# Attention stage of a fused attention and feed-forward kernel: every product takes more than 64 rows and 128 columns of the array

## The chip, the cores and the metric

The kernel runs on one core of one Trainium2 chip. The metric is the device time of one execution in microseconds (us), lower is better. The core has TensorE (PE), with its weight loads shown as PEld, VectorE (DVE), ScalarE (ACT), GpSimd (POOL), and SyncE (SP), which here issues almost all DMAs, in order.

## The reference

Three stages in float32: causal attention with a bias from a running sum of `s`, a feed-forward with softplus, and a normalised, gated feed-forward. Only the first is touched.

```python
# q, k, v: (4, 8, 576, 64); s: (4, 8, 576)
scores = scale * np.matmul(q, k.transpose(0, 1, 3, 2))
s_pos = np.maximum(s, 0.0)
cum = np.cumsum(s_pos, axis=-1)
bias = -(cum[:, :, :, None] - cum[:, :, None, :])
scores = np.where(causal, -1000000000.0, scores + np.minimum(bias, 0.0))
scores = scores - np.max(scores, axis=-1, keepdims=True)
attn = np.exp(scores)
attn = attn / (np.sum(attn, axis=-1, keepdims=True) + 1e-09)
return np.matmul(attn, v).astype(np.float32)
...
x = np.ascontiguousarray(attn_out.transpose(0, 2, 1, 3)).reshape(B * S, H * D)
x = _moe_ref(x=x, **moe_kwargs)
return _moe2_ref(x=x, **moe2_kwargs)
```

## The kernel before

There are 32 heads of 576 positions and 64 channels, worked in 16 pairs. The queries of a head stand in blocks 0 to 3 of 128, and the last 64 queries of both heads of a pair stand together in one block 4 (tile `e4`: rows 0 to 63 the even head, 64 to 127 the odd one). The order of the work is a table of numbers, `OFF`: each step has an offset, an event of head n stands at n plus that offset, all events are sorted, and each engine gets its instructions in that order. Nothing is scheduled afterwards: every engine works its list from the top, waiting where it must. A *slot* is the work between one head's steps and the same steps of the next. Even heads carry the steps of a pair.

The steps of one head, with their names in the table:

- LD, LV: SP loads q, k and v of a pair (L338, L345, L348). QT: TensorE transposes q, then k (`kn`), 96 rows at a time (L357). QH and QL split them into two float32r parts (`hl`), on ACT and DVE.
- QD: SP copies parts of `hl` into the stacked operand `sk` (three DMAs of 256 KB, L381), and four rows of the running sum beside them (L382). QB does the same for block 4: `a8`, 8 rows (L387), and `bd`.
- S0, S1: scores of blocks 0 to 3 (L418, L419, 68 and 128 rows) with the causal mask (L420). S4: scores of block 4 of the pair: a product of `a8`, which has 8 rows (L427), three with `bd` (L428 to L430) and the mask (L431), for columns 0 to 255 and again for 256 to 575.
- M, E, R, N: row maximum (DVE), exponential (ACT), reciprocal (DVE), scaling (POOL, L472).
- T0 to T3: TensorE transposes the weights `e` to PSUM (`pt`, two buffers, shared by all four). T0 and T1 are the six blocks of early queries. T2 and T3 are the late queries (blocks 3 and 4): each block of 128x128 (L504) is followed by one of `e4` in which the head has only 64 rows (L501).
- H copies `pt` to SBUF (ACT, L515), and L takes the remainder (DVE, L521): `ph`, `pl`.
- V0: early queries times v in float32 (L530); the stationary operand is one head's 64 columns, so its output stands in 64 partitions, and both heads share one PSUM tile, `o0`. Each product shows as two in the trace. V1: late queries times v in float32r, eight products over 128 keys and two over the last 64 keys (L539).
- OX, OC, OF, WS, WT: copies out of PSUM and stores of the two parts of the output, `x` (L565) and `xb` (L569).

In the same order stand twelve chunks of the first feed-forward's weights, one per pair for the first twelve pairs: a fetch of 512 KB (`raw`, L222), the conversion, and the split. After the attention the two feed-forwards follow.

Of the kernel before, what the change touches and what calls it, by code (L numbers as in the profile page):

```python
# [8 lines left out]
F32 = mybir.dt.float32  # L9
F32R = mybir.dt.float32r  # L10
# [4 lines left out]
AF = mybir.ActivationFunctionType  # L15
ALU = mybir.AluOpType
# [66 lines left out]
    "V1": 3.16992,  # L83
    "OC": 3.43645,
    "OF": 4.01001,
    "OX": 2.90176,
    "WS": 3.80066,
    "WT": 4.18994,
    "C0": 0.26268,
# [51 lines left out]
def attention_moe_kernel(ctx, tc, q, k, v, s, w_in, w_out, w_gate, w_val, w_out2, rms_g, out):  # L141
    nc = tc.nc
    B, H, S, D = q.shape
# [3 lines left out]
    P = 128  # L147
# [4 lines left out]
    T = 384  # L152
# [19 lines left out]
    pools = {}  # L172
# [4 lines left out]
    def ps_p(name):  # L177
        return ps.tile([P, 512], F32, tag="p", name=name, bufs=2)

    def ps_1(tag, w=512):  # L180
        return ps.tile([P, w], F32, tag=tag, name=tag, bufs=1)

    def f32(ap):
        return ap.bitcast(F32)

    ident = const.tile([P, P], F32, tag="ident", name="ident")
    ident16 = const.tile([P, P], BF16, tag="ident16", name="ident16")
    mask16 = const.tile([P, P], BF16, tag="mask16", name="mask16")
    mask64 = const.tile([P, 64], BF16, tag="mask64", name="mask64")
    bds = []  # L190
    ones = const.tile([P, P], F32R, tag="ones", name="ones")
    gcol = const.tile([P, KD], F32, tag="gcol", name="gcol")
    aug = dram.tile([NH, 4, 2, S], F32R, tag="aug", name="aug")
    aug4 = dram.tile([NH, 4, P + S], F32R, tag="aug4", name="aug4")
# [146 lines left out]
    def a_loadv(p):  # L341
        b, h = pair_bh(p)
        t = pools["nat"].tile([P, NB, 2, D], F32, tag="vn", name="vn", bufs=3)
        for hd in range(2):
            nc.sync.dma_start(  # L345
                out=t[:, 0:4, hd, :],
                in_=v[b, h + hd, 0:512, :].rearrange("(c p) d -> p c d", p=P))
        nc.sync.dma_start(  # L348
            out=t[:, 4], in_=v[b, h:h + 2, 448:576, :].rearrange("h p d -> p h d"))
        st["vn", p] = t  # L350

    def a_qt(p, which):
# [30 lines left out]
        st["sk", n] = sk  # L383

    def a_qb(p):
        a8 = pools["stack"].tile([8, P + S], F32R, tag="a8", name="a8", bufs=2)
        nc.sync.dma_start(out=f32(a8), in_=f32(aug4[2 * p:2 * p + 2]).rearrange("h r n -> (h r) n"))  # L387
        bd, hl = bds[p % 2], st["hl", p]
        for r in (slice(0, 64), slice(64, P)):
            nc.vector.tensor_copy(out=bd[r, :, r], in_=f32(hl[r, 0:2, 512:S]))  # L390
        st["a8", p] = a8

    def a_vh(p):
        vn = st["vn", p]
# [11 lines left out]
    EO = {0: 0, 1: 128, 2: 384, 3: 768}  # L406
# [13 lines left out]
            nc.tensor.matmul(t[:, c + w - P:c + w], ident16, mask16, start=False, stop=True)  # L420

    def a_s4(p):
        a8, bd, hl = st.pop(("a8", p)), bds[p % 2], st["hl", p]
        t = st["s4", p] = ps_s("s4")[:, 0:256], ps_s("s4")[:, 0:320]
        for o, j0, w in ((t[0], 0, 256), (t[1], 256, 320)):
            j = slice(j0, j0 + w)
            nc.tensor.matmul(o, a8[:, 0:P], a8[:, P + j0:P + j0 + w], start=True, stop=False)  # L427
            nc.tensor.matmul(o, bd[:, 0], hl[:, 2, j], start=False, stop=False)  # L428
            nc.tensor.matmul(o, bd[:, 0], hl[:, 3, j], start=False, stop=False)
            nc.tensor.matmul(o, bd[:, 1], hl[:, 2, j], start=False, stop=(j0 == 0))  # L430
        nc.tensor.matmul(t[1][:, 256:320], ident16, mask64, start=False, stop=True)  # L431
# [47 lines left out]
    def a_n4(p):  # L479
        scale_rows(st["e4", p], st["r4", p])  # L480

    # groups of transposed blocks: (key block, query blocks); the first two feed float32 products
    GRP = [
        [(0, [0, 1, 2])],
        [(1, [1, 2]), (2, [2])],
        [(0, [3, 4]), (1, [3, 4]), (4, [4])],
        [(2, [3, 4]), (3, [3, 4])],
    ]
    GW = [384, 384, 448, 384]
    IS = 384  # L490

    def a_t(n, g):
        e, e4, hd = st["e", n], st["e4", n // 2], n % 2
        t = ps_p("pt")
        o = 0
        for jb, ibs in GRP[g]:
            j0 = B0[jb]
            for ib in ibs:
                if ib == 4:
                    r = slice(hd * 64, hd * 64 + 64)  # L500
                    nc.tensor.transpose(t[:, o:o + 64], e4[r, j0:j0 + P], ident[r, r])  # L501
                    o += 64
                else:
                    nc.tensor.transpose(t[:, o:o + P], e[:, EO[ib] + j0:EO[ib] + j0 + P], ident)  # L504
                    o += P
        st["pt", n, g] = t[:, 0:o]

    def a_h(n, g):
        t = st["pt", n, g]
        if g == 0:  # L510
            st["p0", n] = pools["pp"].tile([P, 768], F32, tag="p0", name="p0")
        if g == 2:
            st["ph", n] = pools["pp"].tile([P, 832], F32R, tag="ph", name="ph")
        dst = st["p0", n][:, 384 * g:384 * g + 384] if g < 2 else st["ph", n][:, 448 * (g - 2):448 * (g - 2) + GW[g]]
        nc.scalar.activation(out=dst, in_=t, func=AF.Copy)  # L515

    def a_l(n, g):
        if g == 2:
            st["pl", n] = pools["pp"].tile([P, 832], F32R, tag="pl", name="pl")
        c = slice(448 * (g - 2), 448 * (g - 2) + GW[g])  # L520
        nc.vector.tensor_tensor(out=st["pl", n][:, c], in0=st["pt", n, g], in1=f32(st["ph", n][:, c]), op=ALU.subtract)  # L521

    def a_v0(n):
        p, hd = divmod(n, 2)
        if hd == 0:
            st["o0", p] = ps_1("o0")
        o = st["o0", p][hd * D:(hd + 1) * D]
        vn, x = st["vn", p], st["p0", n]
        for jb, (c, w) in enumerate(((0, 384), (384, 256), (640, 128))):
            nc.tensor.matmul(o[:, IS - w:IS], vn[:, jb, hd, :], x[:, c:c + w], start=(jb == 0), stop=(jb == 2))  # L530

    def a_v1(n):
        p, hd = divmod(n, 2)
        vs = st["vs", p]
        t = st["o1", n] = st["x1"][:, 256:448]
        for i, x in enumerate((st["ph", n], st["pl", n])):
            for jb, c in ((0, 0), (1, 192), (2, 448), (3, 640), (4, 384)):
                r, w = (slice(0, P), 192) if jb < 4 else (slice(64, P), 64)
                nc.tensor.matmul(t[:, 192 - w:192], vs[r, jb, 2 * hd:2 * hd + 2, :].rearrange("p a d -> p (a d)"),  # L539
                                 x[r, c:c + w], start=(i == 0 and jb == 0), stop=(i == 1 and jb == NB - 1))  # L540

    def halves(hd):
        return (slice(0, 64), slice(64, P)) if hd == 0 else (slice(64, P), slice(0, 64))

    def a_ox(p):
        st["x", p] = pools["xo"].tile([P, IS], F32, tag="x", name="x")
        nc.scalar.activation(out=st["x", p], in_=st.pop(("o0", p))[:, 0:IS], func=AF.Copy)

    def a_oc(n):
        a, b_ = halves(n % 2)  # L550
# [20 lines left out]
    def on_pair(fn, hd):  # L571
        def run(n):
            p = n // 2
            if n % 2 == hd and p < NP:
                fn(p)
        return run
# [5 lines left out]
        "R": a_r, "QB": on_pair(a_qb, 0), "S4": on_pair(a_s4, 0), "M4": on_pair(a_m4, 0), "E4": on_pair(a_e4, 0),  # L582
        "R4": on_pair(a_r4, 0), "N4": on_pair(a_n4, 0),
        "N0": lambda n: a_n(n, 0), "N1": lambda n: a_n(n, 1),
        **{f"T{g}": (lambda n, g=g: a_t(n, g)) for g in range(4)},
        **{f"H{g}": (lambda n, g=g: a_h(n, g)) for g in range(4)},
        **{f"L{g}": (lambda n, g=g: a_l(n, g)) for g in range(2, 4)},
        "V0": a_v0, "V1": a_v1, "OC": a_oc, "OF": a_of,
        "OX": on_pair(a_ox, 1), "WS": on_pair(a_ws, 1), "WT": on_pair(a_wt, 1),
        "LD": on_pair(a_load, 0), "LV": on_pair(a_loadv, 0),  # L590
        "QT": lambda n: a_qt(n // 2, n % 2), "QH": lambda n: a_qh(n // 2, n % 2), "QL": lambda n: a_ql(n // 2, n % 2), "QD": a_qd,
        "VH": on_pair(a_vh, 0), "VL": on_pair(a_vl, 0),
# [242 lines left out]
    with tc.manual_schedule():  # L835
        nc.scalar.preload_act_table_set("natural_log_exp_and_others")
        with ExitStack() as es:
# [6 lines left out]
            for c in range(NA):  # L844
                x = OFF["C0"] + OFF["CR"] * c
# [13 lines left out]
        with ExitStack() as es0:  # L859
# [15 lines left out]
            x = OFF1["P0"]  # L875
# [5 lines left out]
            for v in sorted({STEPS[i][0] for i in NS}):  # L881
                i = min(i for i in NS if STEPS[i][0] == v)
                t, n = v % NTILE, FA if v < NTILE else F1 - FA
                if v > 0:
                    for a in range(KD):
                        x = i + OFF1["xs"] + OFF1["xt"] * a
                        at(x + OFF1["xl"], x_load, v, a)
                        at(x, x_split, v, a, nc.gpsimd)
                e = i + n - 1 + OFF1["Y"]
# [6 lines left out]
                x = "5" if t == NTILE - 1 else ""  # L896
# [9 lines left out]
            for c in range(NA, 3 * F2):  # L906
                x = OFF2["L0"] + OFF2["LR"] * c
# [49 lines left out]
```

## Time and profile before

| | |
|---|---|
| time, three runs | 1238.71, 1239.92, 1243.12 us; median 1239.92 |
| profiled execution | span 1242.4 us from the first to the last instruction; no other time of it is listed |
| PE busy | 1176.2 us (95%), 6404 products |
| DVE, ACT, POOL busy | 771.7, 617.7, 471.5 us |
| mean granted TensorE clock | 0.989 of full speed |
| attention's products | from 5.5 us to 314.6 us of the span |

The profiled execution's span is inside the range of the three runs, 2.5 us over the median. Busy times of PE come from a model of pipelined products: a product shown as 0.27 us long may be followed by the next after 0.11 us. What a product really takes is the step from its start to the next one's start.

### The profile page before, as it was taken

Reading aid. Unit: us, or ns where it says so; the run is one execution under the profiler, and the core shown is the slowest. Engines: PE = TensorE matmul, PEld = TensorE weight load, DVE = VectorE, ACT = ScalarE, POOL = GpSimd, SP = SyncE. Lnnn points to the kernel's source line nnn. Section 1 sums busy time; section 2 is a strip of 40 time slices with the busy share of each in tenths; the row PEclk is TensorE's granted clock in tenths of the full one; section 3 lists DMA queues with packets and bytes.
Section 4 is the critical chain, followed back from the end, with each engine's and each line's share of the span. In section 5 each row is a group of like instructions: output and inputs, shape, how many; then the busy total and the mean of one; then the engine's idle time right before and its main releaser. Section 6 shows DMA issues by size and latency. Waiting matters only on the chain.

```text
span 1242.4 us, 18308 instructions
## 1 busy us (share of the span) xinstructions
PE 1176.2 (95%) x6404; PEld 1042.1 (84%) x6404; DVE 771.7 (62%) x1396; ACT 617.7 (50%) x1467; POOL 471.5 (38%) x487
## 2 busy tenths in 40 slices
PE   4999999999999998999989879999999999999998
PEld 3677777776988888999888768899999999999997
DVE  4666676654699999998999999533333332333322
ACT  2667666665677777866666666442121121212111
POOL 4455655543354544346576776762000000000000
PEclk9999999999899998999999999999999999999999
DMA  9998888753333343544452332331101010010000
GB/s 181 198 192 178 200 193 186 167 131 100 99 129 119 122 139 123 162 140 134 159 165 91 120 101 85 117 97 58 39 14 39 14 39 1 14 39 13 26 1 26
DMA packets 139037, 128.96 MB, mean 104 GB/s; under 512 B 66656, under 2 KB 116352, under 8 KB 138912
## 3 DMA queue, kind: packets, MB, share of 16 engines
q1 hardware_dynamic: 138848, 127.74, 38.6%
q8 instruction: 51, 0.84, 0.3%
q14 instruction: 42, 0.34, 0.1%
q0 software_dynamic: 96, 0.04, 0.0%
HBM read 76.46 MB, written 26.12 MB: 83 GB/s over the span
## 4 chain that ended last, share of the span: by engine, by line
PE 67%; DVE 22%; ACT 4%; issue 3%; DMA 2%; SPq 2%; POOL 1%; DVEq 0%; POOLq 0%; ACTq 0%
DVE gl L694 5%; PE x L539 4%; PE pt L504 4%; PE g L644 4%; PE g L643 4%; PE v L644 4%; PE v L643 4%; PE v L642 4%; PE g L642 4%; PE o L530 4%; DVE l L685 4%; DVE e L677 3%; PE o L818 3%; PE o L819 3%; PE o L817 3%
## 5 line engine op out<-in xcount | busy, mean ns | idle before, releaser
L643 PE MATMUL y<-gl,w 128*128 128x384 f32 x384 | 134.5, 350 | 25.4 <-DVE gl L694 24.1
L252 POOL TENSOR_TENSOR wf<-ur 128x512 int32<-128x512 int32 x68 | 94.3, 1386 | 123.7 <-DVE ur L246 34.1
L802 DVE TENSOR_TENSOR u<-g,u 128x384 f32<-128x384 f32 x71 | 39.5, 556 | 158.9 <-ACT u L801 158.9
L642 PE MATMUL y<-gh,w 128*128 128x384 f32 x384 | 130.8, 341 | 3.1 <-ACT l L669 1.4
L644 PE MATMUL y<-gh,w 128*128 128x384 f32 x384 | 130.6, 340 | 0.0
L472 POOL TENSOR_SCALAR e<-e,r 128x256 f32<-128x256 f32 (+2 forms) x144 | 78.3, 560 | 127.9 <-ACT hl L368 103.1
L804 ACT ACTIVATE gh<-l 128x384 fp32r<-128x384 f32 x72 | 37.8, 524 | 156.0 <-DVE l L803 156.0
L801 ACT ACTIVATE u<-g 128x384 f32<-128x384 f32 x71 | 34.8, 490 | 151.9 <-PE g L644 151.8
L643 PEld LDWEIGHTS y<-gl,w 128*128 128x128 f32 x384 | 73.3, 191 | 36.7 <-DVE gl L694 35.1
L643 PE MATMUL g<-xl,w 128*128 128x384 f32 x284 | 95.6, 336 | 1.8 <-DVE xl L636 1.8
L689 ACT ACTIVATE gh<-l 128x384 fp32r<-128x384 f32 x96 | 49.9, 520 | 93.7 <-DVE l L685 93.5
L642 PE MATMUL g<-xh,w 128*128 128x384 f32 x284 | 95.8, 337 | 0.7 <-ACT xh L635 0.7
L694 DVE TENSOR_TENSOR gl<-l,gh 128x384 fp32r<-128x384 f32 x90 | 93.1, 1035 | 4.5 <-ACT gh L689 0.7
L644 PE MATMUL g<-xh,w 128*128 128x384 f32 x284 | 95.9, 338 | 0.0
L642 PE MATMUL h<-xh,w 128*128 128x384 f32 x256 | 89.2, 348 | 6.8 <-DVE e L681 6.6
L642 PE MATMUL v<-xh,w 128*128 128x384 f32 x284 | 94.9, 334 | 0.0
L644 PE MATMUL v<-xh,w 128*128 128x384 f32 x284 | 94.9, 334 | 0.0
L643 PE MATMUL v<-xl,w 128*128 128x384 f32 x284 | 94.9, 334 | 0.0
L643 PE MATMUL h<-xl,w 128*128 128x384 f32 x256 | 88.4, 345 | 3.5 <-POOL xl L639 3.3
L644 PE MATMUL h<-xh,w 128*128 128x384 f32 x256 | 87.4, 341 | 0.0
L685 DVE TENSOR_TENSOR l<-l,e 128x384 f32<-128x384 f32 x96 | 84.0, 875 | 3.7
L677 DVE SCALAR_TENSOR_TENSOR e<-u,e 128x384 f32<-128x384 f32 x96 | 73.9, 770 | 17.1 <-ACT l L669 17.1
(191 smaller groups left out, 3281.7 us busy)
## 6 DMA issues: line engine op xcount, KB each, us to landing
sk<-hl SPq DMA_DIRECT2D x96, 256.0 KB
raw<-in_moe_w_out_dram SPq DMA_DIRECT2D x28, 512.0 KB
raw<-in_moe_w_in_dram SPq DMA_DIRECT2D x16, 512.0 KB
raw<-in_moe_w_gate_dram SPq DMA_DIRECT2D x12, 512.0 KB
raw<-in_moe_w_val_dram SPq DMA_DIRECT2D x12, 512.0 KB
wf<-wf SPq DMA_DIRECT2D x24, 256.0 KB
wl<-wf SPq DMA_DIRECT2D x24, 256.0 KB
xr<-x SPq DMA_DIRECT2D x28, 192.0 KB
```

The lines of the kernel that those rows point to most:

```text
L252: nc.gpsimd.tensor_tensor(out=w.bitcast(I32), in0=u, in1=r3, op=ALU.add)
L472: nc.gpsimd.tensor_scalar(out=e, in0=e, scalar1=r, scalar2=1.0, op0=ALU.mult, op1=ALU.mult)
L504: nc.tensor.transpose(t[:, o:o + P], e[:, EO[ib] + j0:EO[ib] + j0 + P], ident)
L530: nc.tensor.matmul(o[:, IS - w:IS], vn[:, jb, hd, :], x[:, c:c + w], start=(jb == 0), stop=(jb == 2))
L539: nc.tensor.matmul(t[:, 192 - w:192], vs[r, jb, 2 * hd:2 * hd + 2, :].rearrange("p a d -> p (a d)"), x[r, c:c + w], start=(i == 0 and jb = ...
L642: nc.tensor.matmul(o, wh, xh, start=start, stop=False)
L643: nc.tensor.matmul(o, wh, xl, start=False, stop=False)
L644: nc.tensor.matmul(o, wl, xh, start=False, stop=stop)
L677: nc.vector.scalar_tensor_tensor(out=e, in0=st.pop(("u", i)), scalar=-1.0, in1=e, op0=ALU.add, op1=ALU.subtract)
L685: nc.vector.tensor_tensor(out=l, in0=l, in1=st.pop(("e", i)), op=ALU.add)
L689: nc.scalar.activation(out=gh, in_=st["l", i], func=AF.Copy)
L694: eng.tensor_tensor(out=gl, in0=st.pop(("l", i)), in1=f32(st["gh", i]), op=ALU.subtract)
```

## The change

All products of the attention now cover more than 64 rows of the array and all 128 columns. The late queries of a pair's block 4 are transposed once for both heads (T3 becomes a step of the pair, four transposes of 128x128; the fifth, over the last key block, is added to T0 of the odd head, in the same PSUM tile). `ph` and `pl` become tiles of the pair, two new steps H4 and L4 copy that fifth block. V0 takes the columns of both heads as its stationary operand and uses one half of its output; its copy OX is made once a head, 64 partitions each. `a8` is two fixed tiles of 128 rows, zeroed once, of which 8 are loaded. The last key block of v holds 64 zero rows above its 64 loaded rows (a POOL memset a pair, and a smaller DMA), so that V1 runs over 128 rows there too. Comments are dropped, and lines move by up to 21.

```diff
-    "OX": 2.90176,
+    "OX": 2.45,
+    "H4": 1.94275,
+    "L4": 1.9428,
...
+            a8 = pools["stack"].tile([P, P + S], F32R, tag=f"a8{i}", name=f"a8{i}", bufs=1)
+            a8s.append(a8)
+            nc.gpsimd.memset(f32(a8), 0.0)
...
+        nc.gpsimd.memset(t[0:64, 4], 0.0)
         nc.sync.dma_start(
-            out=t[:, 4], in_=v[b, h:h + 2, 448:576, :].rearrange("h p d -> p h d"))
+            out=t[64:P, 4], in_=v[b, h:h + 2, 512:S, :].rearrange("h p d -> p h d"))
...
-        a8 = pools["stack"].tile([8, P + S], F32R, tag="a8", name="a8", bufs=2)
-        nc.sync.dma_start(out=f32(a8), in_=f32(aug4[2 * p:2 * p + 2]).rearrange("h r n -> (h r) n"))
+        a8 = a8s[p % 2]
+        nc.sync.dma_start(out=f32(a8[0:8]), in_=f32(aug4[2 * p:2 * p + 2]).rearrange("h r n -> (h r) n"))
...
     def a_t(n, g):
-        e, e4, hd = st["e", n], st["e4", n // 2], n % 2
+        e = st["e", n]
...
-                if ib == 4:
-                    r = slice(hd * 64, hd * 64 + 64)
-                    nc.tensor.transpose(t[:, o:o + 64], e4[r, j0:j0 + P], ident[r, r])
-                    o += 64
-                else:
-                    nc.tensor.transpose(t[:, o:o + P], e[:, EO[ib] + j0:EO[ib] + j0 + P], ident)
-                    o += P
+                c = EO[ib] + B0[jb]
+                nc.tensor.transpose(t[:, o:o + P], e[:, c:c + P], ident)
+                o += P
+        if g == 0 and n % 2:
+            nc.tensor.transpose(t[:, o:o + P], st["e4", n // 2][:, B0[4]:S], ident)
+            st["pt", n - 1, 4] = t[:, o:o + P].rearrange("p (h q) -> p h q", h=2)
         st["pt", n, g] = t[:, 0:o]
+    def a_t4(p):
+        t = ps_p("pt")
+        for jb in range(4):
+            nc.tensor.transpose(t[:, jb * P:(jb + 1) * P], st["e4", p][:, B0[jb]:B0[jb] + P], ident)
+        st["pt", 2 * p, 3] = t.rearrange("p (b h q) -> p b h q", b=4, h=2)
...
     def a_v0(n):
...
-        o = st["o0", p][hd * D:(hd + 1) * D]
+        o = st["o0", n] = ps_1("o0")
...
-            nc.tensor.matmul(o[:, IS - w:IS], vn[:, jb, hd, :], x[:, c:c + w], start=(jb == 0), stop=(jb == 2))
+            nc.tensor.matmul(o[:, IS - w:IS], vn[:, jb].rearrange("p h d -> p (h d)"), x[:, c:c + w],
+                             start=(jb == 0), stop=(jb == 2))
...
     def a_v1(n):
...
-                r, w = (slice(0, P), 192) if jb < 4 else (slice(64, P), 64)
-                nc.tensor.matmul(t[:, 192 - w:192], vs[r, jb, 2 * hd:2 * hd + 2, :].rearrange("p a d -> p (a d)"),
-                                 x[r, c:c + w], start=(i == 0 and jb == 0), stop=(i == 1 and jb == NB - 1))
+                c = slice(0, W3) if jb < 4 else slice(P, W3)
+                nc.tensor.matmul(t[:, c], vs[:, jb, 2 * hd:2 * hd + 2, :].rearrange("p a d -> p (a d)"),
+                                 x[:, jb, hd, c], start=(i == 0 and jb == 0), stop=(i == 1 and jb == NB - 1))
...
+    def a_ox(n):
+        p, hd = divmod(n, 2)
+        if hd == 0:
+            st["x", p] = pools["xo"].tile([P, IS], F32, tag="x", name="x")
+        r = slice(hd * D, (hd + 1) * D)
+        nc.scalar.activation(out=st["x", p][r], in_=st.pop(("o0", n))[r, 0:IS], func=AF.Copy)
```

TensorE, an even head's slot from T2 to V1. In these lists a digit behind a name is the number of a buffer, and sizes are those of the output. Before:

```order
L504 MATMUL pt<-ident,e 128x128
L501 MATMUL pt<-ident,e_2067 128x64
L504 MATMUL pt<-ident,e 128x128
L501 MATMUL pt<-ident,e_2067 128x64 x2
L530 MATMUL o_2138<-p_2117,vn 64x384
L530 MATMUL o_2138<-p_2117,vn 64x256
L530 MATMUL o_2138<-p_2117,vn 64x128
L504 MATMUL pt<-ident,e 128x128
L501 MATMUL pt<-ident,e_2067 128x64
L504 MATMUL pt<-ident,e 128x128
L501 MATMUL pt<-ident,e_2067 128x64
L539 MATMUL x_188<-ph,vs 128x192 x4
```

And now, the same place (in an odd head's slot the four rows of L513, block 4 of the pair, are not there):

```order
L503 MATMUL pt<-ident,e 128x128 x4
L545 MATMUL o_3777<-p_3758,vn 128x384
L545 MATMUL o_3777<-p_3758,vn 128x256
L545 MATMUL o_3777<-p_3758,vn 128x128
L513 MATMUL pt<-ident,e_3726 128x128 x4
L555 MATMUL x_192<-ph,vs 128x192 x4
L555 MATMUL x_192<-ph,vs 128x64
```

Full and half transposes no longer alternate; nothing else moved on TensorE except the one transpose that joins T0 of odd heads.

GpSimd at the program's start. Before:

```order
L298 MEMSET bd_133 128x256
L298 MEMSET bd_135 128x256
L310 MEMSET rows 32x576 x4
L312 MEMSET zero 32x256
L315 DMA aug_82<-zero 16x4x64 x2
```

And now:

```order
L300 MEMSET bd_133 128x256
L303 MEMSET a_135 128x704
L300 MEMSET bd_137 128x256
L303 MEMSET a_139 128x704
L315 MEMSET rows 32x576 x4
L317 MEMSET zero 32x256
L320 DMA aug_82<-zero 16x4x64 x2
```

Two memsets of 128x704 now stand ahead of that of `rows`, which goes to DRAM as `aug` and from there into every `sk`.

ScalarE, from the odd head's first copies on (the tile `p` is `p0`, what V0 reads). Before:

```order
L515 ACTIVATE p_3373<-pt 128x384 x2
L449 ACTIVATE e,z<-s,m 128x128
L449 ACTIVATE e,z<-s,m 128x512
L449 ACTIVATE e,z<-s,m 128x384
L449 ACTIVATE e,z<-x_188,m 128x256
```

And now:

```order
L530 ACTIVATE p_3197<-pt 128x384 x2
L535 ACTIVATE ph<-pt 128x2x64
L454 ACTIVATE e,z<-s,m 128x128
L454 ACTIVATE e,z<-s,m 128x512
L454 ACTIVATE e,z<-s,m 128x384
L454 ACTIVATE e,z<-x_192,m 128x256
```

The copy H4 (128x2x64) stands between T0's and T1's copies and the exponentials of the next head; its remainder L4 on DVE follows it, and only then is that PSUM buffer free. SP's list has the same DMAs in the same order; one of them, of v, has half its rows.

## Rows read from the trace of the kernel before

**Rows 1.** Stretches: busy of each engine (instructions), granted clock, DMA share, GB/s.

```profile
43.86:222.21 178.35, 178.35 (x1072) 127.40 (x1072) 120.18 (x331) 115.77 (x361) 100.72 (x139) 0.99 0.88 190
222.21:276.80 54.59, 54.59 (x323) 39.08 (x323) 32.72 (x92) 33.74 (x107) 27.57 (x39) 0.97 0.65 147
276.80:312.90 36.10, 34.71 (x192) 23.83 (x193) 16.88 (x45) 19.82 (x59) 12.18 (x20) 1.00 0.38 94
```

**Rows 2.** Waits from 100 to 260 us: who for whom, us, times, longest.

```profile
DVE m L436 <- PE s L420: 28.5, 20, 1.6
ACT p L515 <- PE pt L504: 24.7, 18, 2.4
```

**Rows 3.** TensorE in time order, one even slot: start, length, line, operation, operands.

```profile
204.68 1.51 PE L530 MATMUL o<-p,vn 128*64 128x384 f32 x6
206.12 0.33 PE L504 MATMUL pt<-ident,e 128*128 128x128 f32 x1
206.37 0.27 PE L501 MATMUL pt<-ident,e 64*128 64x64 f32 x1
...
207.03 0.92 PE L539 MATMUL x<-ph,vs 128*128 128x192 f32 x5
...
208.73 0.33 PE L418 MATMUL s<-sk 68*128 68x128 f32 x1
...
210.15 0.83 PE L504 MATMUL pt<-ident,e 128*128 128x128 f32 x6
210.74 0.36 PE L418 MATMUL x<-sk 68*128 68x256 f32 x1
...
211.13 0.67 PE L357 MATMUL qkT<-ident,qn 96*128 96x96 f32 x6
211.63 0.27 PE L504 MATMUL pt<-ident,e 128*128 128x128 f32 x1
...
212.56 1.51 PE L530 MATMUL o<-p,vn 128*64 128x384 f32 x6
```

**Rows 4.** TensorE in time order: S1 and S4 of the next, odd slot.

```profile
218.62 0.36 PE L418 MATMUL x<-sk 68*128 68x256 f32 x1
...
219.10 0.38 PE L427 MATMUL s<-a 8*128 8x256 f32 x1
219.42 0.39 PE L428 MATMUL s<-hl,bd 128*128 128x256 f32 x1
219.64 0.28 PE L429 MATMUL s<-hl,bd 128*128 128x256 f32 x1
219.76 0.28 PE L430 MATMUL s<-hl,bd 128*128 128x256 f32 x1
...
220.89 0.69 PE L357 MATMUL qkT<-ident,kn 96*128 96x96 f32 x6
```

**Rows 5.** ScalarE, 43.86 to 222.21 us, by shape: count, busy us, mean ns.

```profile
L515 ACT ACTIVATE ph<-pt 128x448 fp32r<-128x448 f32 x20 | 11.5, 573 | 0.0
L547 ACT ACTIVATE x<-o 128x384 f32<-128x384 f32 x10 | 4.9, 490 | 0.2
```

**Rows 6.** GpSimd in time order at the start.

```profile
2.95 0.75 POOL L298 MEMSET bd<- 128x256 f32 x2
3.65 2.45 POOL L310 MEMSET rows<- 32x576 f32 x4
```

**Rows 7.** SP's waits, 43.86 to 222.21 us.

```profile
SPq L381 <- ACT e L457: 22.0, 11, 2.6
```

**Rows 8.** SP's waits, 222.21 to 276.80 us.

```profile
SPq L381 <- ACT e L457: 9.6, 4, 2.6
SPq L569 <- DVE xb L561: 7.1, 3, 3.2
```

**Rows 9.** Two more stretches, columns as in rows 1.

```profile
26.52:43.86 17.34, 16.27 (x77) 11.23 (x77) 10.55 (x30) 9.65 (x32) 8.05 (x12) 1.00 1.16 202
185.52:204.75 19.23, 19.23 (x108) 13.80 (x109) 12.12 (x34) 11.75 (x38) 10.20 (x15) 0.91 0.86 178
```

More of the change, by code (lines that the diff above doesn't have):

```diff
@@ L189, in attention_moe_kernel @@
     mask64 = const.tile([P, 64], BF16, tag="mask64", name="mask64")
-    bds = []
+    bds, a8s = [], []
     ones = const.tile([P, P], F32R, tag="ones", name="ones")
@@ L390, in a_qb @@
             nc.vector.tensor_copy(out=bd[r, :, r], in_=f32(hl[r, 0:2, 512:S]))
-        st["a8", p] = a8
     def a_vh(p):
@@ L422, in a_s4 @@
     def a_s4(p):
-        a8, bd, hl = st.pop(("a8", p)), bds[p % 2], st["hl", p]
+        a8, bd, hl = a8s[p % 2], bds[p % 2], st["hl", p]
         t = st["s4", p] = ps_s("s4")[:, 0:256], ps_s("s4")[:, 0:320]
@@ L485, in attention_moe_kernel @@
         [(1, [1, 2]), (2, [2])],
-        [(0, [3, 4]), (1, [3, 4]), (4, [4])],
-        [(2, [3, 4]), (3, [3, 4])],
+        [(0, [3]), (1, [3]), (2, [3]), (3, [3])],
     ]
-    GW = [384, 384, 448, 384]
     IS = 384
+    W3 = S - IS
     def a_t(n, g):
-        e, e4, hd = st["e", n], st["e4", n // 2], n % 2
+        e = st["e", n]
         t = ps_p("pt")
@@ L496, in a_t @@
         for jb, ibs in GRP[g]:
-            j0 = B0[jb]
             for ib in ibs:
-                if ib == 4:
-                    r = slice(hd * 64, hd * 64 + 64)
-                    nc.tensor.transpose(t[:, o:o + 64], e4[r, j0:j0 + P], ident[r, r])
-                    o += 64
-                else:
-                    nc.tensor.transpose(t[:, o:o + P], e[:, EO[ib] + j0:EO[ib] + j0 + P], ident)
-                    o += P
-        st["pt", n, g] = t[:, 0:o]
-    def a_h(n, g):
[L509 to L515, printed above, removed]
+                c = EO[ib] + B0[jb]
@@ new lines, in late, with late_in @@
+    def late(nm, n, g):
+        x = st[nm, n // 2]
+        if g == 2:
+            return x[:, 0:4, n % 2, 0:P]
+        return x[:, 0:4, :, P:W3] if g == 3 else x[:, 4, :, P:W3]
+    def late_in(n, g):
+        t = st["pt", n, g]
+        return t.rearrange("p (b q) -> p b q", b=4) if g == 2 else t
+    def a_h(n, g):
+        if g < 2:
+            if g == 0:
+                st["p0", n] = pools["pp"].tile([P, 768], F32, tag="p0", name="p0")
+            nc.scalar.activation(out=st["p0", n][:, IS * g:IS * g + IS], in_=st["pt", n, g], func=AF.Copy)
+            return
+        if ("ph", n // 2) not in st:
+            for nm in ("ph", "pl"):
+                st[nm, n // 2] = pools["pp"].tile([P, NB, 2, W3], F32R, tag=nm, name=nm)
+        nc.scalar.activation(out=late("ph", n, g), in_=late_in(n, g), func=AF.Copy)
@@ L517, in a_l @@
     def a_l(n, g):
[L518 to L521, printed above, removed]
+        nc.vector.tensor_tensor(out=late("pl", n, g), in0=late_in(n, g), in1=f32(late("ph", n, g)), op=ALU.subtract)
     def a_v0(n):
         p, hd = divmod(n, 2)
-        if hd == 0:
-            st["o0", p] = ps_1("o0")
@@ L535, in a_v1 @@
         t = st["o1", n] = st["x1"][:, 256:448]
-        for i, x in enumerate((st["ph", n], st["pl", n])):
-            for jb, c in ((0, 0), (1, 192), (2, 448), (3, 640), (4, 384)):
-                r, w = (slice(0, P), 192) if jb < 4 else (slice(64, P), 64)
-                nc.tensor.matmul(t[:, 192 - w:192], vs[r, jb, 2 * hd:2 * hd + 2, :].rearrange("p a d -> p (a d)"),
-                                 x[r, c:c + w], start=(i == 0 and jb == 0), stop=(i == 1 and jb == NB - 1))
+        for i, x in enumerate((st["ph", p], st["pl", p])):
+            for jb in range(NB):
+                c = slice(0, W3) if jb < 4 else slice(P, W3)
+                nc.tensor.matmul(t[:, c], vs[:, jb, 2 * hd:2 * hd + 2, :].rearrange("p a d -> p (a d)"),
+                                 x[:, jb, hd, c], start=(i == 0 and jb == 0), stop=(i == 1 and jb == NB - 1))
     def halves(hd):
         return (slice(0, 64), slice(64, P)) if hd == 0 else (slice(64, P), slice(0, 64))
-    def a_ox(p):
-        st["x", p] = pools["xo"].tile([P, IS], F32, tag="x", name="x")
-        nc.scalar.activation(out=st["x", p], in_=st.pop(("o0", p))[:, 0:IS], func=AF.Copy)
+    def a_ox(n):
[4 more added lines that the diff above has]
+        nc.scalar.activation(out=st["x", p][r], in_=st.pop(("o0", n))[r, 0:IS], func=AF.Copy)
     def a_oc(n):
@@ L584, in attention_moe_kernel @@
         "N0": lambda n: a_n(n, 0), "N1": lambda n: a_n(n, 1),
-        **{f"T{g}": (lambda n, g=g: a_t(n, g)) for g in range(4)},
-        **{f"H{g}": (lambda n, g=g: a_h(n, g)) for g in range(4)},
-        **{f"L{g}": (lambda n, g=g: a_l(n, g)) for g in range(2, 4)},
+        **{f"T{g}": (lambda n, g=g: a_t(n, g)) for g in range(3)}, "T3": on_pair(a_t4, 0),
+        **{f"H{g}": (lambda n, g=g: a_h(n, g)) for g in range(3)},
+        "H3": on_pair(lambda p: a_h(2 * p, 3), 0), "H4": on_pair(lambda p: a_h(2 * p, 4), 1),
+        "L2": lambda n: a_l(n, 2),
+        "L3": on_pair(lambda p: a_l(2 * p, 3), 0), "L4": on_pair(lambda p: a_l(2 * p, 4), 1),
         "V0": a_v0, "V1": a_v1, "OC": a_oc, "OF": a_of,
-        "OX": on_pair(a_ox, 1), "WS": on_pair(a_ws, 1), "WT": on_pair(a_wt, 1),
+        "OX": a_ox, "WS": on_pair(a_ws, 1), "WT": on_pair(a_wt, 1),
         "LD": on_pair(a_load, 0), "LV": on_pair(a_loadv, 0),
```

## The prediction

> **What bounds the kernel now.** I first read the stretches of the attention [rows 1]. In the one from 43.86 to 222.21 us, ten pairs of heads that also carry a weight chunk each, PE is busy for all of its 178.35 us. DVE, ACT and POOL are busy for 67, 65 and 56%. The next three pairs, without chunks, are the same picture at 54.59 us. Then the view of waits [rows 2]: DVE and ACT wait for PE, and no wait of PE stands among the long ones. So PE's list sets the end here: 17.8 us a pair, 17.7 without the one half-clock stretch.
>
> But "busy" is not work. In time order [rows 3] a step is what counts, from one start to the next. Six full transposes in a row, each with its own weight load, take 0.11 us a step (0.83 less the last one's 0.27, over five). In the next group a full transpose starts at 206.12 and the half-height one after it at 206.37: 0.25 us, though less is moved. The group of four ends 0.91 us after it began, at 207.03, where 0.44 would do at full height. Wherever a half-height, 8-row or half-width product meets a full one, PE loses 0.09 to 0.15 us: it empties before the shape of the next product can enter. The 96- and 68-row products have no such loss, and the change keeps them.
>
> **The change on PE, per pair.** I take 0.11 us as the step of a full product of up to 256 columns (below).
>
> - T2: 211.63 to 212.56 [rows 3], 0.93 us now; four steps, 0.44. Two heads: 0.98 saved.
> - T3: 206.12 to 207.03, 0.91 for each head; now once a pair, plus one step in T0: 0.55. 1.82 - 0.55 = 1.27 saved.
> - V1: 207.03 to 208.73, 1.70; ten products at full height, 1.10. Two heads: 1.20 saved.
> - V0: 204.68 to 206.12, 1.44. Its columns stay the same, and a stationary operand twice as wide is not shown in float32 by any row. Lower bound of the saving: nothing. Upper: the exit, 0.20 to 0.11, and as much again at the entry. I take 0.14, nearest to the exit's drain; two heads 0.28.
> - S4 with the S1 ahead of it: 218.62 to 220.89 [rows 4], 2.27; S1 alone is 0.39 (210.74 to 211.13 [rows 3]). So S4 takes 1.88. The step from 219.10 to 219.42 is 0.32, the next 0.22, and only from 219.64 to 219.76 it is 0.12, the undisturbed one. Four at 0.12, four of 320 columns at 0.15 (scaled from 0.12, an estimate) and the mask at 0.04 give 1.12. 0.76 saved.
>
> Together 4.5 us a pair: PE's floor falls from 17.7 to 13.2 us. If PE alone counted, that would be 72 us over 16 pairs.
>
> One rule speaks against the wide operands. In six full-height transposes with a load each, the step is 0.11 us [rows 3], so loads lie under the product before. The Trainium skill, "TensorE: Matmul & The Clock Gate", Part 3, says that a weight load overlaps running products only when their row groups differ; by that no load would be hidden once every product takes all rows. The trace disagrees with it here. It stands among the rivals.
>
> **What takes over.** Other engines get little more to do. Per pair ACT has 115.77 / 10 = 11.6 us [rows 1]. OX is split: one more of up to 0.49 us [rows 5]. The copies of late queries go from 448 + 384 elements for each head (1664) to 512 + 512 + 512 + 128 for the pair; by 0.573 us for 448 that is about +0.1. So ACT is at 12.1 to 12.2. DVE has 12.0, its L copies about +0.1. POOL has 10.1 and one small memset. All are under 13.2, ACT by only 8%.
>
> SP's list is the same, and nearly full. In the ten pairs its one long wait is the first `sk` copy of a pair, which needs k's high part, so it waits for PE's k transposes: 22.0 us in 11 waits, 2.0 a pair [rows 7]. Without it SP needs 17.8 - 2.0 = 15.8 us a pair. The DMA engines agree: a share of 0.88 [rows 1] of 17.8 us is 15.7 us of all sixteen. When PE runs ahead, this wait goes, but no more: PE then waits for `sk` at S0. What is late next is the copy behind the weight chunk, in the same queue. The other bound is throughput: 190 GB/s now, and the fullest stretch, with a share of 1.16, moved 202 [rows 9]. At 202 a pair needs 17.8 x 190 / 202 = 16.8 us. I take 16.0, nearer to SP's own row, since a share over 1 contains packets that wait for each other.
>
> - Ten pairs with chunks: 178.35 - 160 = 18.4 us saved. Bounds: 10.4 (16.8) and 44 (13.4, PE).
> - Three pairs without: SP's two long waits are 9.6 / 4 = 2.4 and 7.1 / 3 = 2.4 a pair [rows 8], so SP's floor is 18.2 - 4.8 = 13.4, and PE's 13.2. With ACT close behind I take 13.9: 54.59 - 41.7 = 12.9 saved (11 to 14.4).
> - The last two pairs [rows 1]: 9 us at 4.5 each. There is no S0 or S4 of a next head to cover the copies, and PE already idles 36.10 - 34.71 = 1.4 us. Half, 5 saved (3 to 9).
> - The start: two memsets ahead of `rows` on POOL. bd's 256 columns take 0.375 each, `rows`' 576 take 0.61 [rows 6]; 704 come to 0.71, 1.4 together. All of SP's later list hangs behind the store of `rows`, which has some cover by the loads of q and k ahead of it; between 0 and 1.4 I take 0.7 lost. The stretch from 26.52 [rows 9] ends with the eleventh of SP's waits, 2.0 us, while the DMA engines are full; I take 1 of it. Net 0.
> - H4 and L4 hold the PSUM buffer that T2 of an odd head needs. S1, S4 and the k transposes stand between, 2.0 us by the terms above, over two copies of 0.49, a small one and its remainder: no loss while that cover stands. In the last pair it is gone; that is in its halving. After the attention nothing is changed.
>
> Sum: 18.4 + 12.9 + 5 = 36.3. The profiled execution has a span of 1242.4 us and becomes 1206; its span lies 2.5 over the median of the runs, and the difference carried to the median gives 1203.6. I say 1203. A change under 0.3%, some 4 us, counts as none.
>
> **Rivals.**
>
> - *The queue gives way* (0.15). SP's issues are stretched by full queues, and the real limit is PE: 13.2 a pair, 13.4 with a half-clock stretch now and then. Saved 44 + 14.4 + 9 = 68: 1172. For it: shares over 1 are possible. Against: 190 GB/s would have to become 253.
> - *DMA saturates earlier* (0.20): 16.8 with chunks, 14.5 without, 3 at the end, so 10.4 + 11.1 + 3 = 24.5: 1215. For it: no stretch shows more than 202 GB/s.
> - *The losses are not from shapes* (0.03), but from these tiles' reads; then nothing moves: 1240. Against: S4 loses the same with other tiles, and the 96-row products lose nothing.
> - *PE, now waiting, gets half the clock* (0.04), slower. The stretch from 185.52 has a mean clock of 0.91 and takes 19.23 instead of 17.68 us [rows 9]: about 3.4 us at half clock cost 1.55. PE's slack against today is 4.5 us a pair, so it decides from the third such stretch in a pair on; at half clock all through, work takes 3.4 / 1.85 = 1.84 times as long, 24 us a pair and some 1330 in all. Against: PE would idle 3 us in 16, in pieces.
> - *Loads are not hidden* (0.02), slower. The 25 transposes and 20 products of V1 with a step of 0.11 would need twice that: 5 us a pair, 18.2 instead of 17.7, 1247. This is the rule above; its turning point is a step of 0.21. The row from 210.15 [rows 3] speaks against it: full height, and 0.11.
>
> **How the numbers follow.** The forecast has 0.56, by itself 1192 to 1211. The range 1181 to 1220 leaves out half of the first rival below and, above, no gain, both slower ones and the worst of the second. Faster 0.91, same 0.03, slower 0.06.
>
> **What would show it.** Right: T2 at 0.44 and V1 at 1.1 us between starts, S4 near 1.1; PE idle before S0 of most heads until the chunks end, released by the DMA of `sk`; SP's wait for k gone, DMA share near 1; a period near 16 us, then near 14; PE's clock as before. Wrong: steps of 0.2 left inside T2 or V1; PE still without gaps at 13 us; SP waiting as now while PE waits for DVE or ACT; a half clock in many pairs.

## The result and the profile after

The changed kernel takes 1257.25 us (median of four runs, 1254.15 to 1262.8); the kernel before took 1239.6 beside it (four runs, 1238.71 to 1243.12). The ratio is 1.0136, with an interval of 1.0104 to 1.0167: slower by 1.4%, where I had forecast 1203 us. The profiled execution took 1255.41 us with a span of 1253.7. Its last product of the attention ends at 327.9 us; before, at 314.7. So the whole loss of 13 us lies in the attention.

What the change does to TensorE is there, almost to the digit. In time order, one slot of the changed kernel from T2 to S4 (start, length, line, operation; the answers to [rows 3, 4]):

```profile
108.41 0.60 PE L503 MATMUL pt<-ident,e 128*128 128x128 f32 x4
108.85 1.46 PE L545 MATMUL o<-p,vn 128*128 128x384 f32 x6
110.15 0.60 PE L513 MATMUL pt<-ident,e 128*128 128x128 f32 x4
110.50 0.72 PE L555 MATMUL x<-ph,vs 128*128 128x192 f32 x5
111.06 0.72 PE L555 MATMUL x<-pl,vs 128*128 128x192 f32 x5
111.62 0.31 PE L423 MATMUL s<-sk 68*128 68x128 f32 x1
...
114.08 0.36 PE L432 MATMUL s<-a 128*128 128x256 f32 x1
...
115.23 0.20 PE L436 MATMUL s<-mask,ident 128*128 128x64 bf16 x1
```

From start to start, T2 takes 0.44 us (0.93 before), V0 1.30 (1.44), V1 1.12 (1.70), and S4 1.15 up to its last mask (1.88 with it). No half-height step is left, and no gap.

But PE now stands still for a quarter of the time. The stretch from 44 to 220 us, and after it two neighbouring pieces of it (columns as in rows 1):

```profile
44.00:220.00 176.00, 132.81 (x885) 113.71 (x884) 103.22 (x282) 99.86 (x315) 87.73 (x127) 0.84 0.78 170
```

```profile
97.09:103.92 6.83, 3.31 (x13) 2.71 (x14) 4.03 (x14) 5.77 (x20) 1.77 (x4) 0.50 0.56 94
103.92:117.57 13.65, 11.51 (x91) 9.95 (x89) 8.02 (x20) 5.97 (x18) 8.50 (x12) 1.00 0.93 195
```

In the same 176 us PE was busy for all of the time before. Now it is busy for 132.81, the DMA share has fallen from 0.88 to 0.78 and the mean granted clock to 0.84: there are pieces at 1.2 GHz in every pair. The six transposes of k that follow each long wait of PE took 0.69 us at [rows 4]; here, in each of the pairs from 61 to 222 us, they take 1.18 or 1.22:

```profile
100.61 1.22 PE L363 MATMUL qkT<-ident,kn 96*128 96x96 f32 x6 [5.62 <-ACT e L454]
```

So nothing is saturated. Something waits in a ring, and the view of waits, 40 to 220 us, shows what (us in total, times, longest; the answer to [rows 2]):

```profile
POOL e L477 <- ACT hl L374: 85.2, 17, 7.3
ACT x L566 <- DMA x<-x: 50.0, 9, 9.2
DVE pl L538 <- ACT ph L535: 40.8, 8, 7.3
PEld qkT L363 <- ACT e L454: 39.9, 8, 7.0
PE qkT L363 <- ACT e L454: 39.0, 8, 6.9
```

One of these five names no engine: OX (L566), ACT's copy into the tile `x`, waits for the DMA that stores the tile `x` of the pair before. That is 5.6 us each time on average. The other four are engines that wait for ACT. The chain of waits in order of time (start, length, what) tells the same story for one pair:

```profile
88.40 0.59 SPq L224
...
89.09 0.64 SPq L387
...
91.55 1.43 SPq L388
...
93.09 4.98 DMA x<-x
...
98.15 0.48 ACT x L566
98.63 0.75 ACT p L530 x2
...
99.55 1.22 ACT e L454 x5
...
101.56 0.49 ACT hl L374
...
102.08 0.82 DVE hl L379 x2
```

SP issues the store at 93.09, behind the odd head's `sk` copies and the weight chunk ahead of them. It lands 4.98 us later. Only then can OX write the only buffer of `x`, and behind OX in ACT's list stand the copies of the transposed weights, the exponentials of the next head, and QH for k (`hl`). SP's next `sk` copies wait for that `hl`, and the next store stands behind them. SP's list (L387 is `sk`, L584 the store):

```profile
89.09 2.42 SPq L387 DMA_DIRECT2D sk<-hl  x3
91.55 1.43 SPq L388 DMA_DIRECT2D sk<-aug  x1
93.09 0.94 SPq L584 DMA_DIRECT2D x<-x  x1
...
102.30 2.11 SPq L387 DMA_DIRECT2D sk<-hl  x3
...
109.49 2.47 SPq L387 DMA_DIRECT2D sk<-hl  x3
112.00 0.82 SPq L388 DMA_DIRECT2D sk<-aug  x1
112.93 1.52 SPq L584 DMA_DIRECT2D x<-x  x1
...
123.52 2.12 SPq L387 DMA_DIRECT2D sk<-hl  x3
```

This closes a ring through three queues: store issued 93.09, landed 98.07, OX, ACT's list to QH at 101.56, `sk` at 102.30, thirteen issues from there on, the next store at 112.93. That is 19.84 us, where PE alone would need about 13. From the first `sk` of a pair to that of the next it is 123.52 - 102.30 = 21.22 us, the longest turn; the mean of the eight pairs from 62.77 to 222.97 us is 20.0, where it was 17.8 before. The three pairs after them, which have no chunk, take 54.6 us in both kernels.

Why did the kernel before not have the ring? It had the one buffer too. Its own ACT and SP lists show the distance:

```profile
101.62 0.49 ACT L547 ACTIVATE x<-o 128x384 f32<-128x384 f32 x1
119.30 0.49 ACT L547 ACTIVATE x<-o 128x384 f32<-128x384 f32 x1
```

```profile
107.77 1.12 SPq L565 DMA_DIRECT2D x<-x  x1
```

```profile
109.16 0.32 ACT L552 ACTIVATE tmp<-x 64x192 f32<-64x192 f32 x1 [1.26 <-PE x L539]
```

OX ran once a pair, in the odd head's slot, and 119.30 - 107.77 = 11.5 us after the store was issued. The change lets the even head's OX write first. In the table that is offset 2.45 of the even slot in place of 2.90 of the odd one. In ACT's list it is one slot earlier: between these two offsets, counted within a slot, ACT has no other step, and in either slot OX stands right behind the copy `tmp` (OC). In the trace of before the even slot's `tmp` ends at 109.48, so an even OX there would come 1.7 us after the store's issue. A store takes 4.98 us to land in the rows above. Of the cover of 11.5 us 1.7 are left, and that is not enough.

### The profile page after: what moved, and what is told of

Its sections match the earlier page's. It is cut to its first block, busy times and chain, and to the rows that moved or that the text cites. A ratio compares the mean times of both kernels' runs of the same rounds, so it can differ in the third digit from the quotient of the medians.

```text
span 1253.7 us, 18127 instructions
## 1 busy us (share of the span) xinstructions
PE 1125.6 (90%) x6324; PEld 1039.2 (83%) x6324; DVE 772.4 (62%) x1396; ACT 619.8 (49%) x1483; POOL 474.4 (38%) x505
## 4 chain that ended last, share of the span: by engine, by line
PE 48%; DVE 25%; ACT 9%; DMA 7%; SPq 5%; issue 4%; POOL 1%; DVEq 0%; ACTq 0%; POOLq 0%
DVE gl L715 5%; DMA x<-x 5%; DVE l L706 4%; PE v L664 4%; PE v L663 4%; PE g L664 4%; PE g L665 4%; PE v L665 4%; PE g L663 4%; DVE e L698 3%; PE o L839 3%; PE o L840 3%; PE o L838 3%; ACT e L454 2%; DVE e L702 2%
## 5 line engine op out<-in xcount | busy, mean ns | idle before, releaser
L663 PE MATMUL h<-xh,w 128*128 128x384 f32 x256 | 87.0, 340 | 6.6 <-DVE e L702 6.1
L665 PE MATMUL h<-xh,w 128*128 128x384 f32 x256 | 85.7, 335 | 0.0
```

The costliest lines, as they stand in the source:

```text
L663: nc.tensor.matmul(o, wh, xh, start=start, stop=False)
L665: nc.tensor.matmul(o, wl, xh, start=False, stop=stop)
```

## The experiments

Theory A: the ring through the one buffer of `x` takes the time, and without it the forecast holds. Its rivals: the wide products cost the time themselves, by clock or loads; or it is the place of OX in ACT's list, and the split into two copies, that costs it. "Before" means a run of the kernel before on the same chip.

**Two tiles x.** The changed kernel, with `ph` and `pl` packed to 1664 columns to make room for a second `x`.

```diff
-            st["x", p] = pools["xo"].tile([P, IS], F32, tag="x", name="x")
+            st["x", p] = pools["xo"].tile([P, IS], F32, tag="x", name="x", bufs=2)
...
-                st[nm, n // 2] = pools["pp"].tile([P, NB, 2, W3], F32R, tag=nm, name=nm)
+                st[nm, n // 2] = pools["pp"].tile([P, 8 * W3 + P], F32R, tag=nm, name=nm)
```

> The changed kernel with a second buffer for the output tile x; the space comes from packing ph and pl (1664 instead of 1920 columns). Theory A (the even head's early OX copy waits until the store of the pair before has landed, and holds ACT's whole list for some 5.5 us a pair): these waits vanish, PE runs against SP's queue, a period near 16 us with weight chunks and near 14 without, time 1195 to 1212. Rival B (PE with idle time gets half the clock, and that is what costs): half-clock stretches stay in most pairs and the time stays above 1240. Rival C (the DMA queue binds at 202 GB/s): 16.8 us a pair, about 1215.

1205.87 us (1203.39 to 1209.1), ratio 0.9705 (0.968 to 0.9729). The ring was the whole loss, and without it the time is within 3 us of the forecast's 1203 (in part by luck, see below). The stretch, PE before two heads, and SP's list:

```profile
44.00:220.00 176.00, 158.16 (x1116) 131.86 (x1116) 132.77 (x361) 130.47 (x406) 110.94 (x162) 0.96 0.95 205
```

```profile
100.55 0.30 PE L423 MATMUL s<-sk 68*128 68x128 f32 x1 [1.57 <-DMA sk<-aug]
...
115.47 0.30 PE L423 MATMUL s<-sk 68*128 68x128 f32 x1 [0.70 <-DMA sk<-aug]
```

```profile
60.98 2.17 SPq L387 DMA_DIRECT2D sk<-hl  x3
...
205.75 2.15 SPq L387 DMA_DIRECT2D sk<-hl  x3
...
249.01 2.08 SPq L387 DMA_DIRECT2D sk<-hl  x3
```

Nine pairs with chunks in 144.8 us are 16.1 us a pair; I had said 16.0. PE waits for `sk` before S0, the DMA share is near 1, and the mean clock is back at 0.96. The Trainium skill, "Trainium Kernel Development and Optimization", Best Practices, says to double-buffer so that DMA and compute overlap; this pair of runs agrees, at 1257 and 1206 us. Here it was a store that needed the second buffer, and not a load.

**OX late again.** The changed kernel with the split OX at its old offset.

```diff
-    "OX": 2.45,
+    "OX": 2.90176,
```

> The changed kernel with one number of the table put back: OX at 2.90176, just behind the store of the pair before (2.80), with one x tile as it is. Theory A: the copy still needs the store to have landed, but asks for it 0.45 of a slot later, some 2.7 us, so about half of the 5.5 us a pair goes: 1218 to 1238. If the offset were nothing to do with it, no change against 1255.

1257.78 us, ratio 1.012 (1.0098 to 1.0142): no gain, and a miss. The waits from 60 to 220 us, one store, and the even OX with the copy behind it:

```profile
ACT x L566 <- DMA x<-x: 43.9, 8, 9.1
```

```profile
114.57 1.20 SPq L584 DMA_DIRECT2D x<-x  x1
```

```profile
119.49 0.48 ACT L566 ACTIVATE x<-o 64x384 f32<-64x384 f32 x1 [4.74 <-DMA x<-x]
119.88 0.85 ACT L530 ACTIVATE p<-pt 128x384 f32<-128x384 f32 x2
```

The number in the table changed, but not the order of the work. OX is a step of ACT alone, and ACT has no other step between 2.45 and 2.90 of a slot; the even OX stands right ahead of the copies `p`, as it does in the changed kernel at 98.15 and 98.63. So ACT does not ask later, this run is the changed kernel once more (1257.25 there), and it says nothing for or against Theory A or on where in the ring OX should stand.

**The split alone.** The kernel before, where only OX is split by heads and moved as in the change; then the same with two tiles `x`.

```diff
-    "OX": 2.90176,
+    "OX": 2.45,
...
+    def a_ox(n):
+        p, hd = divmod(n, 2)
+        if hd == 0:
+            st["x", p] = pools["xo"].tile([P, IS], F32, tag="x", name="x")
+        r = slice(hd * D, (hd + 1) * D)
+        nc.scalar.activation(out=st["x", p][r], in_=st["o0", p][r, 0:IS], func=AF.Copy)
```

> The kernel before with the copy OX alone as in the changed kernel: once a head, 64 partitions each, at offset 2.45, one x tile. All products stay. Theory A: ACT waits for the landed store in each pair here too, by up to 5 us less what the slower PE list covers: 1245 to 1290, with the wait of ACT for the DMA of x in the view of waits. Theory B (clock after PE's idle time, no matter whose) has nothing that starts the idle time here: 1240, at most 1244 for the longer ACT list.

> The kernel before with OX split by heads and moved as in the change, and two tiles x in place of one: the counterpart of the run that had one tile and took 1280. Theory A (the one buffer, not the split or the place of OX, is the cost): 1238 to 1248 us, as the kernel before. Rival (ACT's order or PSUM's early release costs by itself): 1255 to 1285 us.

With one tile 1280.45 us, ratio 1.0279 (1.0235 to 1.0323); with two 1244.99, ratio 1.0016 (1.0 to 1.0032). The wait of ACT for the store with one tile, from 60 to 220 us: 3.9 us each, near the 3.3 by which the store's 4.98 us exceed the 1.7 left. With two tiles there is none. Then the stretch with one tile, and with two:

```profile
ACT x L550 <- DMA x<-x: 23.2, 6, 6.1
```

```profile
44.00:220.00 176.00, 162.53 (x858) 112.90 (x857) 99.69 (x265) 96.22 (x296) 82.63 (x115) 0.87 0.75 158
```

```profile
44.00:220.00 176.00, 176.00 (x1049) 126.24 (x1048) 117.20 (x320) 117.39 (x358) 99.05 (x136) 0.98 0.92 191
```

Without any wide product the same loss appears, and the buffer alone takes it away. So it is neither the wide products nor the order on ACT. The part of the change that costs is the split OX, 2.8% by itself; that the whole change loses only 1.4% means, by subtraction, that the rest of it gives back about half.

**The other way to open the ring.** The changed kernel with its one tile, and the store issued earlier: by ACT right behind the odd head's OX, or by SP from an earlier place in its list.

```diff
-    "WS": 3.80066,
+    "WS": 2.46,
...
-        nc.sync.dma_start(out=xT[b][h * D:(h + 2) * D, 0:IS], in_=st.pop(("x", p)))
+        nc.scalar.dma_start(out=xT[b][h * D:(h + 2) * D, 0:IS], in_=st.pop(("x", p)))
```

> The changed kernel with one tile x as it is; the store of a pair's x is issued from ACT's own queue right after the odd head's OX, and not by SP behind the next pair's sk copies. Theory A (the loop of OX, store and sk copies through the one buffer of x costs the time): the store starts some 12 us earlier and has landed before OX of the next pair's even head, ACT's wait for DMA x is below 1 us a pair, and the time comes to 1203 to 1220 us, near the run with two buffers (1206). If instead the number of buffers itself mattered in another way (packed ph and pl, other addresses), 1245 to 1260.

The second has only the first hunk:

> The changed kernel with one tile x; the store stays on SP and one number of the order moves it from slot 3.80 to 2.46, behind OX of the odd head and ahead of a8, v and the odd sk copies of the same pair in SP's list. Theory A: the store is issued a slot earlier, most of ACT's wait for DMA x (about 6 us a pair) goes, 1205 to 1228 us. Rival: SP, which takes its list in order, now stands at the store until OX of the odd head has run and the copies behind it start late; then the wait only changes its engine, 1235 to 1260 us.

From ACT 1212.7 us, ratio 0.9761 (0.9743 to 0.9779); from SP 1206.32, ratio 0.9702 (0.9688 to 0.9716). The second changes one number of the table against the changed kernel, and nothing else. Its stretch, and its two OX of a pair:

```profile
44.00:220.00 176.00, 157.26 (x1111) 131.77 (x1111) 133.38 (x358) 129.67 (x402) 110.68 (x161) 0.96 1.01 205
```

```profile
99.98 0.48 ACT L566 ACTIVATE x<-o 64x384 f32<-64x384 f32 x1 [0.90 <-DMA x<-x]
107.69 0.48 ACT L566 ACTIVATE x<-o 64x384 f32<-64x384 f32 x1
```

The rival of that run, that SP itself would stand at the store, did not come true.

**Part of the wide products alone.** The kernel before with `a8` over 128 rows (S4) and V1's last key block over 128 rows with zero rows; transposes, V0 and OX as before.

```diff
+            a8 = pools["stack"].tile([P, P + S], F32R, tag=f"a8{i}", name=f"a8{i}", bufs=1)
...
-                r, w = (slice(0, P), 192) if jb < 4 else (slice(64, P), 64)
+                r, w = slice(0, P), 192 if jb < 4 else 64
```

> The kernel before with two parts of the change alone: the a8 operand of S4 padded to 128 rows, and V1 over 128 rows with zero rows of v. Transposes, V0 and all copies stay as before. If the losses on PE come from products of different shapes meeting, S4 loses 0.76 and two V1 1.2 us a pair, the period falls from 17.7 to 15.7 with PE still dense or SP's queue just binding: 1207 to 1222. If the losses lie in these tiles' reads: no change, 1240.

1221.41 us (1218.12 to 1222.66), ratio 0.9824 (0.9804 to 0.9844). So the shape losses are real and on the path: 1.8%, some 20 us. In its trace S4 takes 1.15 us to its last mask, and V1 takes 1.14 (1.70 before), though only two of V1's ten products have changed. PE's list is 1.8 us a pair shorter; the period from 59.98 to 209.07 us is 16.6, only 1.2 shorter, at a DMA share of 0.95.

**What bounds it at 16 us.** My forecast named SP's queue and the DMA engines together. Three runs part them. First, on the run with two tiles: `aug`'s four rows as four issues (six more issues a pair, the same bytes), and the third `sk` copy done twice (more bytes).

```diff
-        nc.sync.dma_start(out=f32(sk[0:4, 0]), in_=f32(aug[n][:, :, 0:512]))
+        for i in range(4):
+            nc.sync.dma_start(out=f32(sk[i:i + 1, 0]), in_=f32(aug[n][i:i + 1, :, 0:512]))
```

```diff
+        nc.sync.dma_start(out=f32(sk[D:P, 1]), in_=hl[:, 1:3][:, :, 0:512])
```

> The run with two buffers of x (1205.9 us, period near 16 us a pair) with the copy of aug's four rows into sk issued as four transfers of one row each: six more issues a pair, the same bytes. If SP's issuing bounds the period (each issue holds SP's queue about 0.5 us or more), a pair takes some 3 us more, 1235 to 1250 us. If the bytes that the DMA engines move bound it (share 0.94 to 0.97 in that run), 1203 to 1212 us.

> The run with two buffers of x with the third copy of a head's kT into sk done twice (the same data twice; 256 KB more a head, 512 KB a pair, two issues more a pair). If the bytes bound the period, at the 201 to 212 GB/s of that run a pair takes some 2.5 us more, 1228 to 1245 us. If SP's issuing bounds it, two issues of about 0.6 us, 1210 to 1222 us. If neither, 1203 to 1209 us.

1250.77 us, ratio 1.0057 (1.0042 to 1.0072), and 1320.17, ratio 1.0619 (1.0601 to 1.0637). The second says nothing on bytes: it writes the same place twice, and SP waits until the first copy has landed, as its waits from 60 to 220 us show:

```profile
SPq L388 <- DMA sk<-hl: 61.0, 13, 6.8
```

The first seems to say that issuing is the bound, but look at its stretch and at SP's four issues:

```profile
44.00:220.00 176.00, 144.30 (x935) 122.00 (x935) 112.46 (x305) 111.10 (x343) 92.55 (x137) 0.88 0.74 172
```

```profile
99.73 3.67 SPq L389 DMA_DIRECT2D sk<-aug  x4
```

The DMA share fell to 0.74. SP's list now stands issue behind issue while the DMA engines idle, so with six more issues SP has become the bound; that doesn't mean it was before. So two cleaner runs, on the run with the early store: one more copy of 256 KB a head into a tile that nothing reads (two issues a pair come with it); and the copy of `aug` into `sk` left out from the fourth head on (later heads then get another head's bias), two issues less at 1% of the bytes.

```diff
+        sx = pools["stack"].tile([P, 512], F32, tag="sx", name="sx", bufs=1)
+        nc.sync.dma_start(out=sx, in_=f32(st["hl", p])[:, 1, 0:512])
```

```diff
-        nc.sync.dma_start(out=f32(sk[0:4, 0]), in_=f32(aug[n][:, :, 0:512]))
+        if n < 3:
+            nc.sync.dma_start(out=f32(sk[0:4, 0]), in_=f32(aug[n][:, :, 0:512]))
```

> The changed kernel with the early store (1206.3 us, DMA share near 1) and, for each head, one more copy of 256 KB from hl into a tile that nothing reads (ph and pl are packed to make room): 512 KB and two issues more a pair, and nothing waits for their landing. If the bytes bound the period, 2.5 us a pair at 205 GB/s, 1230 to 1248 us. If SP's issuing bounds it, two issues of 0.6 to 0.7, 1213 to 1228 us. If neither, 1204 to 1210.

> The changed kernel with the early store, where the copy of aug's four rows into sk is left out from the fourth head on (the three sk tiles stand fixed and keep the rows of the first three heads, so the gate's bias of later heads is that of another head): two issues of about 0.9 to 1.3 us and 32 KB less a pair, 1% of the bytes. If SP's issuing bounds the period, some 2 us a pair less, 1172 to 1190 us. If the bytes bound it, 1202 to 1207 us.

1233.71 us (1231.03 to 1234.1) with the bytes added, against 1206.32 without them; 1206.69 (1205.15 to 1207.34) with the issues taken away. The two stretches, bytes added first:

```profile
44.00:220.00 176.00, 145.78 (x987) 123.19 (x986) 118.45 (x318) 114.83 (x354) 97.93 (x145) 0.92 0.99 210
```

```profile
44.00:220.00 176.00, 157.18 (x1121) 130.04 (x1120) 135.36 (x363) 130.85 (x406) 111.40 (x163) 0.98 1.01 204
```

Taking issues away gives nothing and adding bytes costs 27 us (0.9909 against 0.9702 by the ratios), so the transfers themselves, at 204 to 210 GB/s, set the 16 us. SP's issues are stretched by them: in nine pairs of 146 us SP stands in issues for 138 us with the copies of `aug`, and for 138 without; the issue of `a8`, to name one, goes from 0.35 to 1.27 us (medians from 44 to 220 us). The 27 us are 1.7 a pair over all sixteen, less than the 2.5 by 205 GB/s. In the pairs with chunks, where the DMA engines are full, the period is 18.4 us with the bytes (63.90 to 211.40 us) and 16.3 without (60.01 to 206.41), so 2.2 a pair, near the 2.5. The three pairs without chunks had a DMA share of 0.87 without the bytes, and so room for a part of them. SP is not far behind, though: six more issues were enough to put it ahead.

## Why the prediction was wrong

The step that failed is in the sentence on ACT: "OX is split: one more of up to 0.49 us". It prices the copy by its length and asks nothing about the tile that it writes. `x` has one buffer, and the split lets the even head write it one slot sooner than before, while the store that must have left it, issued late behind the `sk` copies, has not landed. I had looked at the other buffer whose life the change alters, H4's and L4's PSUM tile, and named its cover; for `x` I had not. The trace of before held all that was needed: the store at 107.77, the OX at 119.30, and the place of the even OX at 109.48, 1.7 us behind the store's issue. What the runs showed in its place is a wait of ACT of 5.6 us a pair for the store, a pair of 20.0 us where I had 16.0, and 1257 us; with a second `x` the wait is gone and the time is 1206. None of my rivals was this one. My slower rivals had a place in PE; this wait stood between ACT, SP and the DMA.

Point by point, with two tiles `x` as the case in which that step is mended:

- **The terms on PE** were right: T2 0.44 forecast and 0.44 measured, V0 1.30 and 1.30, V1 1.10 and 1.12, S4 1.12 and 1.15 to the start of its last mask. One reading was too narrow: I gave 0.09 to 0.15 us for each meeting of shapes, but the 8-row product's step of 0.32 against 0.12 loses 0.20. The sum used the steps themselves and does not depend on it.
- **What takes over** was right once the ring is open: 16.0 us forecast and 16.1 measured for a pair with a chunk; 13.9 and 14.4 for the three after that, (249.01 - 205.75) / 3. The attention's last product ends at 277.4 instead of 314.7 us, 37.3 earlier; the sum was 36.3. That this is so close is in part luck, twice. I took 16.0 because it was nearer to SP's own row, but the runs show that bytes set it, not issues. And the parts miss in opposite directions: the pairs with chunks end 16.5 us earlier (205.75 for 222.21) where I had 18.4, the next three save 11.3 (12.9), and the last stretch 9.5, where I had 5 and at most 9.
- **DMA saturates earlier**: what binds is what it named, and its rate of 202 GB/s is near the measured 205 (208 over the nine pairs alone), but its period of 16.8 was too long by 0.7.
- **The queue gives way**: no. It needed 253 GB/s; over the stretch of 176 us the fullest run moved 210.
- **Half the clock while PE waits**: it happened, in every pair, and I had given it little. But where the ring is open, the mean clock is back at 0.96 to 0.98 over the stretch, and the time with it. So the low clock comes with the long waits and goes with them. The Trainium skill, "TensorE: Matmul & The Clock Gate", "HAM oscillation — how this bites in real kernels", describes a loop of products that waits for a DMA in each turn and falls to half the rate each time; the piece from 97.09 us, clock 0.50 with PE busy for 3.31 of 6.83 us, agrees, though here PE waits for ACT and ACT for the DMA. How much of the 20 us a pair the low clock adds was not tried by itself.
- **Loads are not hidden**: no. Steps of 0.11 us hold with every load at full height, in the changed kernel too.
- **The losses are not from shapes**: no, by the run with S4 and V1 alone.

## What to carry to other kernels

When an edit splits an operation or moves its first part earlier, ask of each tile that it writes when the last reader of its previous contents is done, stores included, and measure that cover in the trace before the edit: from the reader's start to the place in the engine's list where the next write will stand. For a store, what is left must be longer than its time to landing. A store that stands late in an in-order queue keeps its tile until it lands; with one buffer, that can tie three queues into a ring whose length no busy time shows. Once it is there, a second buffer or the store issued earlier opens it: both took 1206 us here. And before a number in a table of offsets is tried, look whether another step of the same engine stands between the old and the new value; if none does, the run tests nothing.

## What was not expected of the hardware

- A store of 192 KB took 4.98 us from issue to landing (3.8 to 6.4 in the other pairs with chunks) where `sk` copies stood ahead of it in the queue and q and k loads behind; the store's issue itself held SP for only 0.94 us.
- An issue's length on SP isn't a fixed price: the copy of `aug` into `sk` held it for 0.82 to 1.43 us in the rows above, and taking two of them away from a pair gave no time back, since others stretched: the issue of `a8` from 0.35 to 1.27 us.
- A DMA share of 0.74 can go with a full queue: with six more issues a pair the DMA engines idled more, and the run still took 44.9 us more than the one with two tiles, 2.8 a pair.
